# Attention scores computed with the keys as rows, exponentials read from PSUM without a shift, and a checked general path behind a branch

## The chip, the core and the metric

The kernel runs on one core of a Trainium2 chip. TensorE (PE) multiplies matrices and writes PSUM, VectorE (DVE) and ScalarE (ACT) work element by element, GpSimd (POOL) issues the gathers and scatters, SyncE (SP) and ACT issue the plain loads. The metric is the device time of one execution in microseconds (us), the median of several.

## The reference, cut to what matters

Attention over chunks of 32 queries feeds a mixture of experts in which each token goes to one expert. B, H, S, D are 4, 8, 768, 64; there are 8 memory keys per head, 8 experts, and F is 1024.

```python
for c in range(nc):                       # chunks of 32 queries
    l_start = max(0, c_start - 16); r_end = min(S, c_end + 8)
    k_full = concat([mem_k, k[:, :, l_start:r_end]]); v_full = ...   # same for v
    scores = (1 / sqrt(64)) * q_c @ k_full.T
    scores = scores - max(scores, axis=-1)
    a = exp(scores)
    a = a / (sum(a, axis=-1) + 1e-09)
    out[:, :, c_start:c_end] = a @ v_full
x = out in the form (B, S, 512)
logits = x @ w_gate                       # (B, S, 8)
local_gate = sigmoid(x @ w_local)         # below 0.5: take a fresh expert, else the one before
e = ...                                   # expert of the token, a scan along s
out[b, s] = softmax(logits)[e] * (relu(x @ w1[e]) @ w2[e])
```

## The kernel before, in words

Everything is fp32. There are two stages, one after the other, in `attention` and `experts`.

**Attention.** The 768 queries of a batch are cut into 8 blocks of 96 (three chunks each), 32 blocks in all. For a block, one band of 128 keys is used for every query: the 8 memory keys and 120 neighbours; a mask sets what a chunk may not see to -1e30. Loads come in units of half a batch (4 blocks): `load` fetches one `qt` of 768 KB, four bands of `kt` (240 KB each, the memory keys are copied in by POOL) and of `vt`, one unit ahead. For each block:

- `scores` (L151): 8 matmuls `s_ps` at L155, one per head, with the queries as the stationary operand (64 rows, 96 columns) and the keys streaming (128 columns). The heads lie in pairs on the two halves of the 128 rows. DVE scales and masks all of it from PSUM to `s_sb` (L159), takes the negated maximum `nmax` (L163), and ACT makes the exponentials head by head, 8 instructions of 96x128, with `nmax` as bias (L165).
- `values` (L168), for each half of the heads: PE transposes `s_sb` into `pt_ps` (L172, four transposes), ACT copies that to `pt` (L174), PE multiplies it with the values, which carry a column of ones, into `o_ps` (L178), and DVE adds 1e-9 to the sums, inverts them and scales (L180 to L182) into `x`.
- `logits` (L186): PE transposes `x` into `xt_ps` (L189), DVE copies it to `xt` (L191), PE multiplies it with the gate's weights into `l_ps` (L194), DVE copies that to `lt` (L195).

The scores of a block are asked for one block ahead, inside a unit. After each batch, `route` (L197) finds the expert of each token: DVE makes a code per token, PE turns the codes into a line (`c_ps`, L222, twice), DVE scans along the 768 tokens (`run` L226, `rank` L233, L237), PE turns the ranks back (`r_ps`, L240), and POOL scatters the rows of `x` to `x_dram` with 8 indirect DMAs, each of which waits for the one ahead of it (L263).

**Experts.** From the counts of tokens a plan of tiles of 128 tokens is made. Each tile gathers its rows (`xs`, L366), loads the two weights of its expert (`w_sb`, 2 MB each, four buffers ahead, L370 and L372), transposes (`g_ps`), multiplies (`h_ps` L391, `y_ps` L396) and scatters the result (`out_dram`, L399). 24 tiles always run; up to 7 more stand in nested branches on the number of tiles, which each engine reads into a register (L360). Here 27 run.

The order of the instructions on each engine is made by a scheduler when the program is built; each engine then works strictly through its own list. PSUM has 8 banks: `s_ps` holds two buffers of two, `pt_ps` two of one, `o_ps` one, and `xt_ps`, `l_ps`, `c_ps` and `r_ps` share one.

Of the kernel before, what the change touches and what calls it, by code (L numbers as in the profile page):

```python
# [15 lines left out]
P = 128  # L16
# [23 lines left out]
WBUF = 4  # L40


GATE = -1.5 * 2.0 ** -23
# [6 lines left out]
@with_exitstack  # L50
def kernel(
    ctx: ExitStack,
    tc: tile.TileContext,
    q: bass.AP,
    k: bass.AP,
    v: bass.AP,
    mem_k: bass.AP,
    mem_v: bass.AP,
    w_gate: bass.AP,
    w_local: bass.AP,  # L60
    w1: bass.AP,
    w2: bass.AP,
    out: bass.AP,
):
    nc = tc.nc
    keep = ctx.enter_context(tc.tile_pool(name="keep", bufs=1))
    dram = ctx.enter_context(tc.tile_pool(name="dram", bufs=1, space=bass.MemoryType.DRAM))
    x_dram = dram.tile([E * REGION, XW], I32, name="x_dram")

    ident = keep.tile([P, P], F32, name="ident")  # L70
    make_identity(nc, ident)
    count = keep.tile([E, 1], F32, name="count")

    attention(tc, q, k, v, mem_k, mem_v, w_gate, w_local, x_dram, ident, count)
    experts(tc, x_dram, out, ident, count, w1, w2)


@with_exitstack
def attention(ctx, tc, q, k, v, mem_k, mem_v, w_gate, w_local, x_dram, ident, count):

    nc = tc.nc
    once = ctx.enter_context(tc.tile_pool(name="once", bufs=1))
    ld = ctx.enter_context(tc.tile_pool(name="ld", bufs=2))
    sp = ctx.enter_context(tc.tile_pool(name="sp", bufs=2))
    xp = ctx.enter_context(tc.tile_pool(name="xp", bufs=2))
    sm = ctx.enter_context(tc.tile_pool(name="sm", bufs=3))
    sps = ctx.enter_context(tc.tile_pool(name="sps", bufs=2, space=PSUM))
    tps = ctx.enter_context(tc.tile_pool(name="tps", bufs=2, space=PSUM))
    ops = ctx.enter_context(tc.tile_pool(name="ops", bufs=1, space=PSUM))
    xps = ctx.enter_context(tc.tile_pool(name="xps", bufs=1, space=PSUM))  # L90

    memk = once.tile([P, B, HP, NMEM], F32, name="memk")
    nc.scalar.dma_start(memk, mem_k)

    def load(b, half):
        qt = ld.tile([P, HP, HQ], F32, name="qt")
        nc.sync.dma_start(qt, q[b, half])
        kt = ld.tile([P, HALF, HP, P], F32, name="kt")
        nc.gpsimd.tensor_copy(kt[:, :, :, 0:NMEM], memk[:, b:b + 1].to_broadcast([P, HALF, HP, NMEM]))
        vt = ld.tile([P, HALF, H * VW], F32, name="vt")  # L100
        for j in range(HALF):
            s0 = band_start(HALF * half + j)
            nc.sync.dma_start(kt[:, j, :, NMEM:P], k[b][:, :, s0:s0 + BAND])
            nc.scalar.dma_start(vt[0:NMEM, j], mem_v[b])
            nc.scalar.dma_start(vt[NMEM:P, j], v[b, s0:s0 + BAND])
        return qt, kt, vt

    units = [(b, half) for b in range(B) for half in range(2)]
    loaded = {units[0]: load(*units[0])}

# [3 lines left out]

    masks = {}
    for name, qb in (("first", 0), ("mid", 1), ("last", NQB - 1)):
        m = masks[name] = once.tile([QB, P], F32, name=f"mask_{name}")
        nc.vector.memset(m, MASKED)
        nc.vector.memset(m[:, 0:NMEM], 0.0)
        for g in range(QB // CHUNK):  # L120
            c0 = QB * qb + CHUNK * g
            lo = max(c0 - LEFT, 0) - band_start(qb) + NMEM
            hi = min(c0 + CHUNK + RIGHT, S) - band_start(qb) + NMEM
            nc.vector.memset(m[CHUNK * g:CHUNK * g + CHUNK, lo:hi], 0.0)

# [23 lines left out]

    def scores(qt, kt, half, j):  # L150
        s_ps = sps.tile([QB, 2, HP, P], F32, name="s_ps")  # L151
        for a in range(HP):
            for u in range(2):
                h = slice(DH * u, DH * u + DH)
                nc.tensor.matmul(s_ps[:, u, a], lhsT=qt[h, a, QB * j:QB * j + QB], rhs=kt[h, j, a],  # L155
                                 start=True, stop=True)
        s_sb = sp.tile([QB, H, P], F32, name="s_sb")
        m = mask_of(HALF * half + j)
        nc.vector.scalar_tensor_tensor(  # L159
            s_sb, s_ps.rearrange("p u a n -> p (u a) n"), SCALE,  # L160
            m.rearrange("p (o n) -> p o n", o=1).to_broadcast([QB, H, P]), ALU.mult, ALU.add)
        nmax = sm.tile([QB, H], F32, name="nmax")
        nc.vector.tensor_reduce(nmax, s_sb, axis=AX.X, op=ALU.max, negate=True)  # L163
        for i in range(H):
            nc.scalar.activation(s_sb[:, i], s_sb[:, i], ACT.Exp, bias=nmax[:, i:i + 1])  # L165
        return s_sb

    def values(s_sb, vt, j, x):  # L168
        for u in range(2):
            pt_ps = tps.tile([P, HP, QB], F32, name="pt_ps")  # L170
            for a in range(HP):
                nc.tensor.transpose(pt_ps[:, a], s_sb[:, HP * u + a], identity=ident[:QB, :QB])  # L172
            pt = sp.tile([P, HP, QB], F32, name="pt")
            nc.scalar.copy(pt, pt_ps)  # L174
            o_ps = ops.tile([QB, HP, VW], F32, name="o_ps")
            for a in range(HP):
                h = 2 * a + u
                nc.tensor.matmul(o_ps[:, a], lhsT=pt[:, a], rhs=vt[:, j, VW * h:VW * h + VW], start=True, stop=True)  # L178
            rinv = sm.tile([QB, HP, 1], F32, name="rinv")
# [6 lines left out]
    def logits(x, lt):  # L186
        xt_ps = xps.tile([P, DK, QB], F32, name="xt_ps", tag="xps")
        for kk in range(DK):
            nc.tensor.transpose(xt_ps[:, kk], x[:, P * kk:P * kk + P], identity=ident[:QB, :QB])  # L189
        xt = sp.tile([P, DK, QB], F32, name="xt")  # L190
        nc.vector.tensor_copy(xt, xt_ps)  # L191
        l_ps = xps.tile([QB, E + 1], F32, name="l_ps", tag="xps")
        for kk in range(DK):
            nc.tensor.matmul(l_ps, lhsT=xt[:, kk], rhs=wg[:, kk], start=(kk == 0), stop=(kk == DK - 1))  # L194
        nc.vector.tensor_copy(lt, l_ps)  # L195
# [70 lines left out]

    for n, (b, half) in enumerate(units):
        if n + 1 < len(units):
            loaded[units[n + 1]] = load(*units[n + 1])
        if half == 0:  # L270
            x = xp.tile([QB, NQB, XW], F32, name="x")
            lt = sm.tile([QB, NQB, E + 1], F32, name="lt")
        qt, kt, vt = loaded.pop((b, half))
        held = scores(qt, kt, half, 0)
        for j in range(HALF):
            ahead = scores(qt, kt, half, j + 1) if j + 1 < HALF else None
            values(held, vt, j, x[:, HALF * half + j])
            logits(x[:, HALF * half + j], lt[:, HALF * half + j])
            held = ahead
        if half == 1:  # L280
            route(b, x, lt)


# [167 lines left out]
```

## Time and profile before

| | us |
|---|---|
| median of 3 runs | 842.08 (836.47 to 842.37) |
| the profiled execution, its own time | 847.82 |
| its span, first to last instruction | 846.1 |
| PE busy | 706.1 |
| DVE busy | 205.1 |
| ACT busy | 160.4 |
| mean granted TensorE clock | 0.749 |

The span is cut into 40 slices of some 21 us on the page; a digit is the busy share of an engine in tenths. The attention takes about the first 17 of the slices. PE runs each fp32 matmul as two passes, so the 256 matmuls of `s_ps` are 512 in the profile, and a transpose as one. A group's line gives engine, operation, tile, shape and count, then busy time and the mean of one in ns, then the idle time ahead of it and what ended it. In the chain of waits each piece is what the end of the program hung on at that time.

### The profile page before, as it was taken

To read this page: it belongs to the slowest core of one execution; us is meant where nothing else is said; L and a number is where in the kernel's file an instruction comes from. 1 tells how busy PE (TensorE), PEld (TensorE's weight loads), DVE (VectorE), ACT (ScalarE), POOL (GpSimd) and SP (SyncE) were. 2 spreads that over 40 slices of the span, in tenths; PEclk is the share of its full clock that TensorE was granted. 3 is DMA by queue.
4 is the path that set the end of the run, shared out by engine and by line. 5 is a ranking of instruction groups with operands and counts; after the bars stand their busy time and mean duration, and the time that the engine had idled before them with its cause. 6 is when DMAs were issued, how large, how long until landed. Compare 5 with 4: busy or idle time off the path is not lost.

```text
span 846.1 us, 10132 instructions
## 1 busy us (share of the span) xinstructions
PE 706.1 (83%) x4064; PEld 556.5 (66%) x4064; DVE 205.1 (24%) x522; ACT 160.4 (19%) x406; POOL 87.8 (10%) x111
## 2 busy tenths in 40 slices
PE   3999898989898977301899999999999999997663
PEld 3788778878887777300686767777686777756551
DVE  3445464547454743600000000000000000000000
ACT  1524233322332341000011111111111111110000
POOL 1000002100200020022010101011010101000000
PEclk9555555555555555555799999999999999997887
DMA  9430405140601010027999988888888888850000
GB/s 249 108 108 28 131 4 170 41 135 10 173 29 51 10 58 10 0 60 293 428 425 423 376 313 323 314 301 326 328 319 321 325 318 300 309 202 23 26 25 3
DMA packets 38273, 156.41 MB, mean 185 GB/s; under 512 B 21261, under 2 KB 21389, under 8 KB 31312
## 3 DMA queue, kind: packets, MB, share of 16 engines
q1 hardware_dynamic: 25824, 127.41, 40.8%
q0 software_dynamic: 6368, 19.72, 6.5%
q10 hardware_dynamic: 6032, 8.61, 3.8%
q8 instruction: 34, 0.56, 0.3%
q14 instruction: 15, 0.12, 0.1%
HBM read 143.11 MB, written 13.39 MB: 185 GB/s over the span
## 4 chain that ended last, share of the span: by engine, by line
PE 61%; issue 13%; DMA 13%; DVE 8%; ACT 1%; POOL 1%; ACTq 0%; POOLq 0%; DVEq 0%
PE h_ps L391 16%; PE y_ps L396 15%; PE o_ps L178 9%; PE s_ps L155 7%; DMA out_dram<-y,to 5%; PE pt_ps L172 5%; PE l_ps L194 4%; DMA xs<-x_dram,rows 3%; PE xt_ps L189 3%; DMA x_dram<-x,row 3%; PE c_ps L222 1%; PE r_ps L240 1%; DVE s_sb L159 1%; DMA vt<-in_v_dram 1%; DVE x L182 1%
## 5 line engine op out<-in xcount | busy, mean ns | idle before, releaser
L391 PEld LDWEIGHTS h_ps<-xt,w_sb 128*128 128x128 f32 x1728 | 204.2, 198 | 15.6 <-DVE xt L380 8.2
L391 PE MATMUL h_ps<-xt,w_sb 128*128 128x128 f32 x1728 | 206.7, 282 | 5.8 <-DVE xt L380 5.0
L396 PE MATMUL y_ps<-w_sb,ht 128*128 128x512 f32 x432 | 189.9, 592 | 0.0
L396 PEld LDWEIGHTS y_ps<-w_sb,ht 128*128 128x128 f32 x432 | 80.0, 190 | 90.4 <-issue 90.4
L178 PE MATMUL o_ps<-vt,pt 128*96 128x65 f32 x512 | 95.1, 364 | 5.8 <-DVE x L182 4.4
L178 PEld LDWEIGHTS o_ps<-vt,pt 128*96 128x96 f32 x512 | 88.2, 277 | 13.9 <-issue 10.6
L382 DVE TENSOR_TENSOR to<-xs,past 128x1 int32<-128x1 f32 x27 | 4.3, 159 | 370.0 <-DMA out_dram<-y,to 224.8
L155 PE MATMUL s_ps<-kt,qt 64*96 64x128 f32 x512 | 78.0, 437 | 13.6 <-POOL place L309 8.0
L165 ACT ACTIVATE s_sb<-s_sb,nmax 96x128 f32<-96x128 f32 x256 | 80.5, 390 | 31.5 <-DVE nmax L163 31.5
L393 ACT ACTIVATE ht<-h_ps 128x512 f32<-128x512 f32 x54 | 32.2, 597 | 270.8 <-PE h_ps L391 270.8
L155 PEld LDWEIGHTS s_ps<-kt,qt 64*96 64x96 f32 x512 | 57.2, 267 | 24.6 <-issue 8.1
L378 PE MATMUL g_ps<-ident,xs 128*128 128x128 f32 x108 | 18.0, 313 | 64.6 <-DMA xs<-x_dram,rows 64.6
L172 PE MATMUL pt_ps<-ident,s_sb 96*128 96x96 f32 x256 | 60.6, 378 | 11.0 <-ACT pt L174 6.9
L399 POOL DMA_INDIRECT out_dram<-y,to x27 | 27.3, 1013 | 386.7 <-ACT y L398 352.7
L378 PEld LDWEIGHTS g_ps<-ident,xs 128*128 128x128 f32 x108 | 14.4, 161 | 73.5 <-issue 64.1
L174 ACT COPY pt<-pt_ps 128x384 f32<-128x384 f32 x64 | 30.5, 478 | 151.8 <-PE o_ps L178 112.3
L172 PEld LDWEIGHTS pt_ps<-ident,s_sb 96*128 96x128 f32 x256 | 44.7, 230 | 21.0 <-ACT pt L174 11.2
L263 POOL DMA_INDIRECT x_dram<-x,row x32 | 29.6, 925 | 247.3 <-DVE x L260 171.6
L398 ACT ACTIVATE y<-y_ps,xs 128x512 f32<-128x512 f32 x27 | 18.6, 688 | 170.9 <-PE y_ps L396 164.6
L194 PEld LDWEIGHTS l_ps<-wg,xt 128*96 128x96 f32 x256 | 44.8, 280 | 1.8 <-DVE xt L191 0.9
L194 PE MATMUL l_ps<-wg,xt 128*96 128x9 f32 x256 | 43.8, 301 | 0.7 <-DVE xt L191 0.7
L163 DVE TENSOR_REDUCE nmax<-s_sb 96x8 f32<-96x1024 f32 x32 | 38.3, 1198 | 0.1
(97 smaller groups left out, 303.0 us busy)
## 6 DMA issues: line engine op xcount, KB each, us to landing
w_sb<-in_w_dram SPq DMA_DIRECT2D x54, 2048.0 KB
vt<-in_v_dram ACTq DMA_DIRECT2D x32, 243.8 KB
kt<-in_k_dram SPq DMA_DIRECT2D x32, 240.0 KB
qt<-in_q_dram SPq DMA_DIRECT2D x8, 768.0 KB
vt<-in_mem_v_dram ACTq DMA_DIRECT2D x32, 16.2 KB
x_dram<-x,row POOLq DMA_INDIRECT x32, 3.2
xs<-x_dram,rows POOLq DMA_INDIRECT x27, 6.8
out_dram<-y,to POOLq DMA_INDIRECT x27, 7.5
```

Of the source, the lines that this page charges most:

```text
L155: nc.tensor.matmul(s_ps[:, u, a], lhsT=qt[h, a, QB * j:QB * j + QB], rhs=kt[h, j, a], start=True, stop=True)
L163: nc.vector.tensor_reduce(nmax, s_sb, axis=AX.X, op=ALU.max, negate=True)
L165: nc.scalar.activation(s_sb[:, i], s_sb[:, i], ACT.Exp, bias=nmax[:, i:i + 1])
L172: nc.tensor.transpose(pt_ps[:, a], s_sb[:, HP * u + a], identity=ident[:QB, :QB])
L174: nc.scalar.copy(pt, pt_ps)
L178: nc.tensor.matmul(o_ps[:, a], lhsT=pt[:, a], rhs=vt[:, j, VW * h:VW * h + VW], start=True, stop=True)
L194: nc.tensor.matmul(l_ps, lhsT=xt[:, kk], rhs=wg[:, kk], start=(kk == 0), stop=(kk == DK - 1))
L263: nc.gpsimd.indirect_dma_start(out=x_dram[:, :], out_offset=bass.IndirectOffsetOnAxis(ap=row[:, n:n + 1], axis=0), in_=x[:, n].bitcast(I32 ...
L378: nc.tensor.transpose(g_ps[:, kk], xs[:, P * kk:P * kk + P], identity=ident)
L391: nc.tensor.matmul(h_ps[:, m], lhsT=w1_sb[:, kk, P * (g + m):P * (g + m) + P], rhs=xt[:, kk], start=(kk == 0), stop=(kk == DK - 1))
L393: nc.scalar.activation(ht[:, g:g + 4], h_ps, ACT.Relu)
L396: nc.tensor.matmul(y_ps, lhsT=ht[:, m], rhs=w2_sb[:, m], start=(m == 0), stop=(m == FK - 1))
```

## The change

The host now lays out, for each of the 32 blocks, its queries, the band of 128 keys with the memory keys in it, and the values in the same way, so that a block is three plain loads (`qt` 196 KB, `kt` 262 KB, `vt` 266 KB), three blocks ahead, in four buffers. The scores of a block are made with the keys as the stationary operand, so that they come out with the keys as rows: the form that the value product needs. ACT reads them from PSUM and writes the exponentials to `pt`, three instructions of 128 rows by 256 elements (one for each chunk of 32 queries, over all heads), with the scale in the instruction and the mask as a bias per key; no maximum is taken off. The transposes `pt_ps`, their copies, the scaling and masking, the maximum and the addition of 1e-9 are gone. `o_ps` of all 8 heads stands in two banks and is inverted by one instruction and scaled by two. The copy of `xt_ps` goes from DVE to ACT. `s_ps` keeps two buffers of two banks, `o_ps` has two banks, `xt_ps` one of its own, and `l_ps`, `c_ps` and `r_ps` share one. All inverted sums are kept, counted at the end of the attention if they lie between 2^-40 and 2^40, and the count goes to a register of each engine after the experts. If it isn't 24576, the whole of attention and experts runs again in the form of before; that second program stands behind the branch.

```diff
     attention(tc, q, k, v, w_gate, w_local, x_dram, ident, count, kept_i)
     experts(tc, x_dram, out, ident, count, w1, w2)
+    kept = nc.values_load(kept_i, min_val=0, max_val=NT * H, skip_runtime_bounds_check_because="a count of sums")
+    with tc.If(kept < NT * H):
+        attention(tc, q, k, v, w_gate, w_local, x_dram, ident, count, None)
+        experts(tc, x_dram, out, ident, count, w1, w2)
...
-    ld = ctx.enter_context(tc.tile_pool(name="ld", bufs=2))
+    ld = ctx.enter_context(tc.tile_pool(name="ld", bufs=4))
...
+    def load(n):
+        qt = ld.tile([P, HP, QB], F32, name="qt")
+        nc.sync.dma_start(qt, q[n])
+        kt = ld.tile([P, HP, P], F32, name="kt")
+        nc.sync.dma_start(kt, k[n])
+        vt = ld.tile([P, H, VW], F32, name="vt")
+        nc.scalar.dma_start(vt, v[n])
         return qt, kt, vt
+    AHEAD = 3
+    loaded = {n: load(n) for n in range(AHEAD)}
...
+    def scores(qt, kt, qb):
+        s_ps = sps.tile([P, 2, 512], F32, name="s_ps")
+        st = s_ps[:, :, 0:HP * QB].rearrange("p u (a n) -> p u a n", a=HP)
         for a in range(HP):
             for u in range(2):
                 h = slice(DH * u, DH * u + DH)
-                nc.tensor.matmul(s_ps[:, u, a], lhsT=qt[h, a, QB * j:QB * j + QB], rhs=kt[h, j, a],
-                                 start=True, stop=True)
+                nc.tensor.matmul(st[:, u, a], lhsT=kt[h, a], rhs=qt[h, a], start=True, stop=True)
+        pt = sp.tile([P, 2, HP, QB], F32, name="pt")
+        m = mask_of(qb)
+        for g in range(NG):
+            c = slice(CHUNK * g, CHUNK * g + CHUNK)
+            nc.scalar.activation(pt[:, :, :, c], st[:, :, :, c], ACT.Exp, bias=m[:, g:g + 1], scale=SCALE)
+        return pt
+    def values(pt, vt, n, x):
+        o_ps = ops.tile([QB, 2, 512], F32, name="o_ps")
+        ot = o_ps[:, :, 0:HP * VW].rearrange("p u (a d) -> p u a d", a=HP)
+        for u in range(2):
+            for a in range(HP):
+                nc.tensor.matmul(ot[:, u, a], lhsT=pt[:, u, a], rhs=vt[:, 2 * a + u], start=True, stop=True)
+        rinv = rinvs[:, n]
+        nc.vector.reciprocal(rinv, ot[:, :, :, DH])
+        for u in range(2):
+            nc.vector.tensor_tensor(
+                x[:, 0:D].rearrange("p (a u d) -> p u a d", u=2, d=DH)[:, u], ot[:, u, :, 0:DH],
+                rinv[:, u].rearrange("p (a o) -> p a o", o=1).to_broadcast([QB, HP, DH]), op=ALU.mult)
...
     def logits(x, lt):
-        xt_ps = xps.tile([P, DK, QB], F32, name="xt_ps", tag="xps")
+        xt_ps = tps.tile([P, DK, QB], F32, name="xt_ps")
...
-        nc.vector.tensor_copy(xt, xt_ps)
+        nc.scalar.copy(xt, xt_ps)
...
+    begun = begin(0)
+    for n in range(NB):
...
+        ahead = begin(n + 1) if n + 1 < NB else None
+        make_values(*begun, n, x[:, j])
+        logits(x[:, j], lt[:, j])
+        begun = ahead
+        if j == NQB - 1:
             route(b, x, lt)
+    if not shifted:
+        flat = rinvs.rearrange("p n u a -> p (n u a)")
+        ok = once.tile([QB, NB * H], F32, name="ok")
+        nc.vector.tensor_scalar(ok, flat, 1.0 / SAFE, None, ALU.is_ge)
+        nc.vector.scalar_tensor_tensor(ok, flat, SAFE, ok, ALU.is_le, ALU.mult)
+        kept = once.tile([QB, 1], F32, name="kept")
+        nc.vector.tensor_reduce(kept, ok, axis=AX.X, op=ALU.add)
...
+        nc.tensor.matmul(k_ps, lhsT=kept, rhs=every, start=True, stop=True)
+        nc.vector.tensor_copy(kept_i, k_ps)
```

The form of before is kept as `shifted_scores` and `shifted_values` for the second program; the route and the experts are unchanged.

How this orders PE in the middle of a batch: the first list is of before, a stretch in the second half of the first batch; a row is one run of matmuls into a tile, with the count of matmuls in the program.

```order
L178 MATMUL o_ps<-vt,pt 96x65 x4
L155 MATMUL s_ps<-kt,qt 96x128 x3
L172 MATMUL pt_ps<-ident,s_sb 128x96 x4
L155 MATMUL s_ps<-kt,qt 96x128 x2
L189 MATMUL xt_ps<-ident,x 128x96 x4
L178 MATMUL o_ps<-vt,pt 96x65 x4
L155 MATMUL s_ps<-kt,qt 96x128 x4
L194 MATMUL l_ps<-wg,xt 96x9 x4
L172 MATMUL pt_ps<-ident,s_sb 128x96 x4
L155 MATMUL s_ps<-kt,qt 96x128 x5
```

The second is of the change, one block in the third batch, with the semaphores that each row waits for; every block there has this pattern.

```order
L183 MATMUL s_ps<-qt,kt 128x96 [waits DMAHW4_49,DMAHW3_49]
L183 MATMUL s_ps<-qt,kt 128x96 x7
L240 MATMUL xt_ps<-ident,x 128x96 [waits DVE_49,PE_49]
L240 MATMUL xt_ps<-ident,x 128x96 x3
L196 MATMUL o_ps<-vt,pt 96x65 [waits DMAHW5_49,PE_49]
L196 MATMUL o_ps<-vt,pt 96x65 x5
L245 MATMUL l_ps<-wg,xt 96x9 [waits Activation_49]
L245 MATMUL l_ps<-wg,xt 96x9 x3
L196 MATMUL o_ps<-vt,pt 96x65 x2
```

The scores in this piece are those of two blocks ahead, `o_ps` is of the next block, `xt_ps` and `l_ps` of the present one; the transposes of the exponentials, which stood at four places of a unit between them, are gone.

ACT in the same place, one block: three exponentials, the copy of `xt_ps`, and the issue of a later block's values, all in one queue.

```order
L188 ACTIVATE pt<-s_ps,mask_last 128x8x32 [waits Activation_49]
L188 ACTIVATE pt<-s_ps,mask_last 128x8x32 x2
L242 COPY xt<-xt_ps 128x384 [waits PE_49,Activation_49]
L109 DMA vt<-in_v_dram 128x520 [waits DMAHW6_49,DMAHW2_49,PE_49]
L188 ACTIVATE pt<-s_ps,mask_first 128x8x32 [waits Activation_49]
```

Before, this queue held 8 exponentials and two copies of `pt_ps` in their place.

PE at the route behind the second batch, in the change:

```order
L183 MATMUL s_ps<-qt,kt 128x96 x9
L273 MATMUL c_ps<-ident,code 8x96 x4
L183 MATMUL s_ps<-qt,kt 128x96 x5
L273 MATMUL c_ps<-ident,code 8x96 x4
L183 MATMUL s_ps<-qt,kt 128x96 x3
L291 MATMUL r_ps<-ones,rank 96x1 x8
L240 MATMUL xt_ps<-ident,x 128x96 x4
L196 MATMUL o_ps<-vt,pt 96x65 x3
L245 MATMUL l_ps<-wg,xt 96x9 x4
L196 MATMUL o_ps<-vt,pt 96x65 x5
L240 MATMUL xt_ps<-ident,x 128x96 x4
```

Three matmuls of the scores stand between the second `c_ps` and `r_ps`, and on DVE the scaling of the block's `x` stands behind the whole scan. At the routes of the first and the third batch, 17 to 22 matmuls of the scores, 10 to 16 of `o_ps` and one or two sets of `xt_ps` stand there.

122 lines of the change are left out of this document (65 added, 57 removed).

## The prediction

> **What bounds the kernel now.** I read first the granted clock in the slices of the page and then the table of stretches, whose bounds I took from the first value product, the last logits, the first scatter of the last batch and the first product of the experts. In a row of the table stand the stretch, its length, the busy time and count of PE, PE's weight loads, DVE, ACT and POOL, then the granted clock, the DMA share and GB/s.
>
> ```profile
> PEclk9555555555555555555799999999999999997887
> ...
> 25.03:339.79 314.76, 282.48 (x1678) 245.75 (x1676) 159.16 (x397) 102.28 (x305) 23.70 (x29) 0.50 0.24 68
> 339.79:358.27 18.48, 6.44 (x36) 5.33 (x36) 12.10 (x39) 0.26 (x1) 0.00 (x1) 0.50 0.00 0
> 358.27:405.80 47.53, 3.29 (x13) 2.18 (x13) 4.58 (x16) 0.00 (x0) 11.16 (x12) 0.50 0.51 192
> 405.80:846.10 440.30, 402.92 (x2256) 294.20 (x2256) 19.63 (x49) 50.81 (x81) 49.64 (x50) 0.96 0.71 271
> ```
>
> The reader is to see four stages. In the first PE is busy 282 of 315 us, at half clock, with DVE at half and ACT at a third of the time: PE sets it. The second is the last route, a chain through DVE. The third is the scatter of the last batch and the first gathers and weights. The fourth is the experts, PE again. The change touches the first stage and what lies ahead of it, adds a little to the second, and puts something behind the fourth. So the next view is the chain of waits over one unit of four blocks.
>
> ```profile
> by line: PE o_ps L178 29.0%; PE s_ps L155 26.4%; PE pt_ps L172 17.6%; PE l_ps L194 12.9%; PE xt_ps L189 8.6%; DVE x L182 2.1%; ACT pt L174 1.3%; issue 1.0%; DVE rinv L181 0.5%; DVE rinv L180 0.5%; DVE lt L195 0.4%; ACTq L174 0.0%
> ...
> 139.61 1.96 PE s_ps L155 x16
> ...
> 143.96 0.90 PE xt_ps L189 x4
> 144.86 1.23 PE o_ps L178 x8
> 146.09 1.20 PE l_ps L194 x8
> ...
> 177.05 1.96 PE s_ps L155 x16
> ```
>
> From 139.61 to 177.05 four blocks take 37.44 us, 9.36 each. 94.5% of it is PE, 17.6% (1.65 us a block) transposes `pt_ps`, and some 5% waits for DVE and ACT.
>
> **The first stage, block by block.** Taken away from PE: 8 transposes a block. Left: 16 passes of `s_ps`, 16 of `o_ps`, 4 of `xt_ps`, 8 of `l_ps`. By the rows above, where they run in one piece: `o_ps` 2 x 1.23 = 2.46, `xt_ps` behind scores 0.90, `l_ps` 1.20. The scores swap their operands. A pass now loads 128 columns instead of 96 and streams 96 instead of 128, which no row shows on 64 rows. Its bounds: if the stream decides, 1.96 x 96/128 = 1.47; if the load decides, 16 passes at the 0.15 us of the experts' first products (128 columns loaded, on 128 rows, at half clock; rows below), 2.4. I take 1.96, the row of the same tile with the same operands. Sum 6.52; the order lists a switch less often than before, and I add 0.1 for handovers: 6.6 a block. The upper bound keeps the whole fragmentation of before: 9.36 less the 17.6% and less the 5.8% of waits, 7.2.
>
> It holds only if nothing else takes longer than PE. ACT: three exponentials and a copy.
>
> ```profile
> 24.75 2.45 ACT L165 ACTIVATE s_sb<-s_sb,nmax 96x128 f32<-96x128 f32 x8
> ...
> L174 ACT COPY pt<-pt_ps 128x384 f32<-128x384 f32 x64 | 30.5, 478 | 151.8 <-PE o_ps L178 112.3 <-PE pt_ps L172 23.1 <-DMA vt<-in_v_dram 8.5
> ...
> L393 ACT ACTIVATE ht<-h_ps 128x512 f32<-128x512 f32 x54 | 32.2, 597 | 270.8 <-PE h_ps L391 270.8
> ...
> L182 DVE TENSOR_TENSOR x<-o_ps,rinv 96x256 f32<-96x256 f32 x64 | 26.6, 416 | 1.1
> ```
>
> Eight exponentials of 128 take 2.45, so 0.306 each; from 384 to 512 elements an ACT instruction grows by 119 ns, 0.93 an element, so 256 cost 0.306 + 0.119 = 0.43, three 1.28, with the copy 1.76 a block of 6.6. DVE has two of 0.42 and an inversion that I put at 0.2 (it is shorter than half of such a row): 1.0, and small copies. In the order of the change, 8 matmuls of scores (1.96) stand between the end of `o_ps` and its `xt_ps`, longer than DVE's 1.0 plus handovers; between `xt_ps` and `l_ps` stand 12 passes of `o_ps`, 1.85, while ACT needs what is left of its exponentials (1.28 less 0.90) and 0.48. So both are covered, ACT by about 1 us: if that cover goes, `l_ps` waits and the block ends at PE plus the lack. The removed work of DVE (scale, mask, maximum) and the second of ACT's copies ran beside PE; I count it only in the waits that go, 0.54 a block, already left out.
>
> Three routes lie inside this stage. Their `c_ps`, twice each, and `r_ps` stay on PE; the rows are those of the last.
>
> ```profile
> 343.52 1.46 PE c_ps L222 x8
> ...
> 352.34 2.68 PE r_ps L240 x16
> ```
>
> 2 x 1.46 + 2.68 = 5.6, three times 16.8. Between the end of the second `c_ps` (344.98) and `r_ps` lie 7.36 us of DVE. At the routes of the first and third batch the order puts 17 to 22 matmuls of scores and 10 or more of `o_ps` there, 6 us and more; I count 1.5 each for what DVE delivers late. At the second only 3 matmuls, 0.8 us, so 6.5 are idle; and since the scaling of that block's `x` is queued on DVE behind the scan, `xt_ps` starts 0.6 late and the next one, with no scores ahead of it, 1.2: 8.3. At the first blocks, before the order is in step, 1.5; at the last three, where no scores are left to cover DVE, 4.2. Waits together 17. The stage: 32 x 6.6, less 3.9 for two scores done ahead of it, plus 16.8 and 17: 241 instead of 315.
>
> **The start.** Loads of half a batch give way to loads of a block.
>
> ```profile
> 0.00:12.00 12.00, 3.35 (x28) 3.03 (x30) 4.21 (x19) 0.00 (x0) 2.97 (x19) 1.00 0.86 235
> ...
> 17.92 1.28 ACT L165 ACT_TABLE_LOAD   x1 [17.92 <-DMA vt<-in_v_dram]
> ...
> 25.03 1.54 PE L178 MATMUL o_ps<-vt,pt 128*96 128x65 f32 x8
> ```
>
> ACT's queue was held by the issue of values until 17.92. Three blocks are now 2.2 MB, 9.3 us at the 235 GB/s of the first stretch, and the issue of the fourth values, which waits for one of the first loads, stands ahead of the table load: I put that at 8, plus 1.28 and the exponentials 1.28, first value product at 11, between 9 and 15, instead of 25.
>
> **The second and third stages.** The check adds three DVE instructions, which run while the last `xt_ps` and `l_ps` do, and in the last route one matmul and one copy: 0.5, so 19. The last eight scatters, the gathers, the weights and the experts keep their order and their waits: nothing. First scatter at 11 + 241 + 19 = 271 instead of 358, 87 less.
>
> **The end.** Each engine reads the count and branches.
>
> ```profile
> L360 POOLq TENSOR_LOAD <-total_i x1: 513/513/513, 760.9 to 760.9; - x1
> ...
> _compat.py:109 PEldq COMPARE_BRANCH  x5: 65/92/3321, 754.6 to 832.7; - x5
> _compat.py:109 POOLq COMPARE_BRANCH  x5: 34/40/50, 761.5 to 838.0; - x5
> ```
>
> POOL is the last to be free there. A read of 0.51 and a branch of 0.04 are the lower bound, 0.55; the 3.32 of PE's longest branch, the one that leaves the last tile, with the read the upper, 3.8. I take 2. The Trainium skill, "Runtime: NRT & Kernel Launch", section "Instruction fetch mechanics", says that a taken branch to a target outside the window already fetched must wait for a fetch; by it the jump over the second program would sit at the upper bound, and the sum would be 2 us more. PE's 3.32 agrees; POOL's 0.05 doesn't show it.
>
> **The sum.** 87 - 2 = 85. The profiled execution's span goes from 846.1 to 761, its time from 847.8 to 763. The median of the runs shown, 842.08, lies 5.7 below that execution, so I forecast 757.
>
> **Rivals.**
>
> *The clock rises in the attention* (8%).
>
> ```profile
> 24.00:36.00 12.00, 12.00 (x79) 10.12 (x76) 7.29 (x13) 6.59 (x21) 0.00 (x0) 0.50 0.45 121
> ...
> 409.00:410.00 1.00, 1.00 (x7) 0.50 1.04 442
> ...
> 412.00:413.00 1.00, 1.00 (x11) 1.00 1.08 459
> ```
>
> The experts' first passes ran at 0.50, about 0.15 us each, and 4 us of them brought the clock to 1.00 and 0.09 to 0.11 a pass. In the attention 12 us of busy PE did not. If a mix without `pt_ps` did, a block would cost about 0.72 x 6.6 = 4.8, with 1.8 x 32 = 58 less: 700. Against it: the stream's share of a pass hardly grows. The Trainium skill, "TensorE: Matmul & The Clock Gate", Part 1, has the clock go to full after about 3.4 us of sustained work, and Part 4 says that transposes don't count as such work in the same way; by these the change, which takes away two thirds of the transposes, could be enough. The row from 24 to 36, with most of its time in other matmuls, speaks against it.
>
> *PE waits for DVE and ACT in each block* (6%). If exponentials from PSUM by strides of 32 cost what the row of a 512-wide one does, 0.6 each, and DVE's handovers take 1 us more, `l_ps` and `xt_ps` come late by 1 to 1.5 a block: 32 to 48 us, 790 to 805.
>
> *Loads take over* (2%), the case that ends slower. ACT's next exponentials are queued behind the issue of a block's values, which waits for loads of some three blocks back. A block is 0.725 MB.
>
> ```profile
> 17.00:18.00 1.00, 0.00 (x0) 1.00 1.07 224
> ```
>
> At the 224 GB/s of a stretch in which the DMA engines were full, that is 3.2 us, under half a block. It would decide from 6.6 us (110 GB/s), and the kernel would be slower than before by 1% from 9.5 us a block, below 77 GB/s, at 855 or more. Larger pieces than before speak against it.
>
> *The change doesn't do what it says* (2%). If the count falls short, the second program runs as well: 757 and about 840, near 1600. The inputs are a tenth of a unit normal, so scores are near 0 and a sum is that of 48 to 64 terms near 1; nothing comes near 2^40. If the swapped scores cost more than the transposes saved, the result is within 1% (2%).
>
> **How the numbers follow.** The forecast has 80%; its own range: low, with the scores at 1.47 (16 less) and the start at 9, 739; high, with 7.2 a block (19 more), the start at 15 and the branch at 3.8, 782. For 8 in 10 I widen the low side for half of a risen clock: 730 to 785. Faster by over 1% (about what a measurement of this kernel can tell from no change) is 0.95: the forecast, the clock and the waits; within 1% 0.02; slower 0.03, the loads and a second program.
>
> **What would show it.** Right: no `pt_ps`; first `o_ps` near 11; a block near 6.6 us in the chain with PE over 95% of it; a clock of 0.50; an idle PE of 6 to 8 us before `r_ps` only at the second route; first scatter of the last batch near 271; 490 us from there to the end. Wrong: `s_ps` passes of 0.15 us or more, `l_ps` idle behind ACT's copy, or an end that stretches by more than 4 us.

## The result, and the profile after

| | before | changed |
|---|---|---|
| median, us | 839.49 (836.47 to 842.37, 4 runs) | 767.77 (766.81 to 768.29, 4 runs) |
| ratio, 95% interval | | 0.9145 (0.9101 to 0.9189) |
| profiled execution, own time and span | 847.82, 846.1 | 768.29, 766.6 |

The changed kernel is faster by 8.6%. The forecast of 757 was 11 us too low; 768 lies inside the range of 730 to 785.

First the same table of stretches as before, now of the changed kernel, with the bounds at the same events: first value product, last logits, first scatter of the last batch, first product of the experts; then the stretch from the issue of the last `out_dram` to the end.

```profile
10.25:254.76 244.51, 231.66 (x1474) 216.05 (x1472) 65.53 (x214) 52.86 (x128) 22.18 (x24) 1.00 0.35 104
254.76:273.19 18.43, 6.56 (x38) 5.42 (x38) 12.09 (x40) 0.26 (x1) 0.00 (x0) 1.00 0.00 0
273.19:321.00 47.81, 4.23 (x17) 3.12 (x18) 4.59 (x16) 0.00 (x0) 11.17 (x12) 1.00 0.53 201
321.00:766.60 445.60, 401.23 (x2253) 292.52 (x2252) 19.64 (x49) 50.80 (x81) 49.34 (x50) 0.96 0.70 267
747.10:766.60 19.50, 0.00 (x0) 0.00 (x0) 0.00 (x0) 0.00 (x0) 0.99 (x1) 0.59 0.02 5
```

The same last stretch of the kernel before:

```profile
833.54:846.10 12.56, 0.00 (x0) 0.00 (x0) 0.00 (x0) 0.00 (x0) 1.00 (x1) 0.65 0.01 2
```

Stage by stage, the span changes by: start 10.25 - 25.03 = -14.8; attention 244.5 - 314.8 = -70.3; last route 0.0; first scatter of the last batch to the last `out_dram` 473.9 - 475.3 = -1.4; end 19.5 - 12.6 = +6.9. Together -79.5, from 846.1 to 766.6.

The chain of waits of the changed kernel behind the second route: start, length, what.

```profile
136.29 1.39 PE c_ps L273 x8
...
138.29 1.76 DVE run L277
...
141.87 1.81 DVE rank L284
...
145.04 2.70 PE r_ps L291 x16
...
158.84 1.96 PE s_ps L183 x16
160.79 0.83 PE xt_ps L240 x4
161.63 1.87 PE o_ps L196 x12
163.50 1.19 PE l_ps L245 x8
164.68 0.73 PE o_ps L196 x4
165.42 1.96 PE s_ps L183 x16
```

A block is now 165.42 - 158.84 = 6.58 us, all of it PE: five runs of passes follow one another without a gap. The 7.36 us of DVE between the end of `c_ps` (137.68) and `r_ps` are there as well; PE works on six passes of the scores at their beginning and is idle for 6.27 of them.

One row of the page looks as if the clock had risen: the attention stood at 5 before, and stands at 9 now.

```profile
PEclk9999999999999999999999999999999999988985
```

But the passes have the same length as before: 1.96 for sixteen of `s_ps`, 1.19 for eight of `l_ps` (1.20 before). Either these passes don't feel the clock, or the row is wrong. The runs below decide that.

### The profile page after: what moved, and what is told of

The parts are those of the page before. It is cut to its first block, busy times and chain, and to the rows that moved or that the text cites. A ratio compares the mean times of both kernels' runs of the same rounds, so it can differ in the third digit from the quotient of the medians.

```text
span 766.6 us, 9247 instructions
## 1 busy us (share of the span) xinstructions
PE 647.7 (84%) x3810; PEld 520.7 (68%) x3810; DVE 103.6 (14%) x332; ACT 106.4 (14%) x214; POOL 85.3 (11%) x106
## 4 chain that ended last, share of the span: by engine, by line
issue 32%; PE 31%; DMA 31%; DVE 3%; POOL 0%; POOLq 0%; ACT 0%; SPq 0%; ACTq 0%; DVEq 0%
DMA out_dram<-y,to 24%; PE o_ps L196 11%; PE s_ps L183 8%; PE l_ps L245 5%; PE xt_ps L240 4%; DMA x_dram<-x,row 3%; DMA xs<-x_dram,rows 3%; PE c_ps L273 1%; PE r_ps L291 1%; DMA kt<-in_k_dram 1%; DVE x L200 1%; DVE rank L284 0%; DVE run L277 0%; POOL out_dram L468 0%; DVE rank L288 0%
## 5 line engine op out<-in xcount | busy, mean ns | idle before, releaser
L183 PE MATMUL s_ps<-qt,kt 64*128 64x96 f32 x512 | 72.1, 435 | 6.8 <-DMA kt<-in_k_dram 6.3
L183 PEld LDWEIGHTS s_ps<-qt,kt 64*128 64x128 f32 x512 | 61.8, 323 | 12.4 <-issue 8.5
L188 ACT ACTIVATE pt<-s_ps,mask_mid 128x256 f32<-128x256 f32 x72 | 29.4, 471 | 68.5 <-PE s_ps L183 35.8
L240 PE MATMUL xt_ps<-ident,x 96*128 96x96 f32 x128 | 29.4, 380 | 5.4 <-DVE x L200 5.3
L242 ACT COPY xt<-xt_ps 128x384 f32<-128x384 f32 x32 | 15.3, 478 | 92.0 <-PE xt_ps L240 88.2
L435 POOL DMA_INDIRECT xs<-x_dram,rows x27 | 26.1, 967 | 11.1 <-issue 8.0
L240 PEld LDWEIGHTS xt_ps<-ident,x 96*128 96x128 f32 x128 | 19.9, 219 | 10.9 <-issue 10.2
```

The costliest lines, as they stand in the source:

```text
L183: nc.tensor.matmul(st[:, u, a], lhsT=kt[h, a], rhs=qt[h, a], start=True, stop=True)
L188: nc.scalar.activation(pt[:, :, :, c], st[:, :, :, c], ACT.Exp, bias=m[:, g:g + 1], scale=SCALE)
L435: nc.gpsimd.indirect_dma_start(out=xs.bitcast(I32), out_offset=None, in_=x_dram[:, :], in_offset=bass.IndirectOffsetOnAxis(ap=rows[:, i:i ...
```

## The experiments

### The end: is the longer end the branch?

The theory was that most of the 6.9 us are steps which POOL takes one after the other at the branch, whose body is skipped. These are the sequencers' rows of line 81 of the changed kernel, the branch: shortest, median and longest in ns, then the first and last start in us.

```profile
L81 POOLq EVENT_SEMAPHORE  x6: 17/30/43, 756.2 to 756.6; - x6
...
L81 PEldq COMPARE_BRANCH  x1: 3820/3820/3820, 746.9 to 746.9; - x1
...
L81 POOLq COMPARE_BRANCH  x1: 55/55/55, 753.4 to 753.4; - x1
L81 POOLq INC_SWDGE_SEM  x1: 1881/1881/1881, 756.7 to 756.7; - x1
```

POOL compares at 753.4, is seen next at 756.2, and is done at 758.6, 8.0 us ahead of the end. Before, POOL's last step of that kind ended at 838.0, 8.1 ahead of the end. The branch's own length on POOL is 0.055 us; the 2.8 us show only as a gap behind it, ahead of its first semaphore step.

The changed kernel was run again beside its variants.

> The changed kernel unaltered, run beside its variants. Both theories: 767 to 768.5 us, a granted clock of 1.00 through the attention, and 19 to 20 us from the issue of the last out_dram (L468) to the end of the span.

Measured 769.69 us (766.47 to 770.74), a little above what was expected; its end took 19.2 us.

**Without the branch.**

```diff
-    kept = nc.values_load(kept_i, min_val=0, max_val=NT * H, ...)
-    with tc.If(kept < NT * H):
-        attention(tc, q, k, v, w_gate, w_local, x_dram, ident, count, None)
-        experts(tc, x_dram, out, ident, count, w1, w2)
```

> The changed kernel without L80 to L83: the count of kept sums is still made and never read, and the general program behind it is left out (the data here don't need it). Theory: the end grew by 6.9 us (19.5 us from the last out_dram to the end of the span, 12.6 before), and 5.8 us of it are POOL's own steps at the untaken branch, one after the other: the read and compare (752.8 to 753.4), the jump (753.4 to 756.2) and the semaphore step with its INC_SWDGE_SEM of 1.88 us (756.2 to 758.6). Without them the end is 12.5 to 14 us and the time 768 - 5.8 = 762. Rival: the longer end isn't the branch's but the last scatter's landing or the code's size elsewhere; then the end stays at 19 and the time at 767 to 768.

Measured 761.02 us (759.99 to 763.13), 8.7 below the run beside it. The last stretch of this kernel, from its last `out_dram`:

```profile
746.55:759.10 12.55, 0.00 (x0) 0.00 (x0) 0.00 (x0) 0.00 (x0) 0.99 (x1) 0.64 0.01 4
```

12.55 against 12.56 before: the whole of the longer end is the branch with what stands behind it. Some 3 us of the difference between the two profiled spans lie elsewhere (the last `out_dram` was issued at 746.55 here, at 749.81 in the run beside it and at 747.10 in the first profile of the changed kernel); that is the spread from one execution to the next.

**A small body behind the branch.**

```diff
     with tc.If(kept < NT * H):
-        attention(tc, q, k, v, w_gate, w_local, x_dram, ident, count, None)
-        experts(tc, x_dram, out, ident, count, w1, w2)
+        nc.vector.memset(count, 0.0)
```

> The same read and the same branch, with one vector memset behind it in place of the general program (which is left out). If the distance of the jump is what costs, POOL's 2.8 us and PE's branch of 3.82 us shrink to under 0.3 us each, the end is 16.5 to 17 us and the time 765. If any branch costs it, nothing changes: 19.5 and 768. If the step with INC_SWDGE_SEM is there only because the body holds DMAs of POOL, it goes as well: 14 us and 762.5.

Measured 762.94 us (761.79 to 764.97). This run doesn't tell the two theories apart: the body writes only `count`, which the experts' plan has read by 271, and the scheduler put the branch ahead of the experts' tiles. Its rows show a branch over a short body, at 271.5 instead of the end.

```profile
L81 POOLq COMPARE_BRANCH  x1: 50/50/50, 271.5 to 271.5; - x1
L81 PEldq COMPARE_BRANCH  x1: 239/239/239, 271.5 to 271.5; - x1
```

In the next two runs the body writes `out`, and the branch stayed at the end.

**One DMA behind the branch, from SP.**

```diff
     with tc.If(kept < NT * H):
-        attention(tc, q, k, v, w_gate, w_local, x_dram, ident, count, None)
-        experts(tc, x_dram, out, ident, count, w1, w2)
+        nc.sync.dma_start(out[0:1, 0:1], ident[0:1, 0:1])
```

> The same read and branch at the end, with one 4-byte DMA of SP to out behind it in place of the general program (which is left out, and so is its need here), so that the branch stays where it was and the jump over its body is short. Theory (the distance costs on PE and POOL): PE's branch 3.82 -> 0.2 to 0.3 us, POOL's step from branch to semaphore 2.8 -> under 0.3 us, and, as POOL issues no DMA in the body, no INC_SWDGE_SEM: the end is 12.6 + 0.6 to 1 for the read = 13.2 to 13.7 us, the time 762 to 763. Rival (any branch at the end costs its 5.8 us): end 18 to 19.5 us, 768.

Measured 761.9 us (761.21 to 763.87). PE's branch and the end in this run:

```profile
L81 PEldq COMPARE_BRANCH  x1: 252/252/252, 748.9 to 748.9; - x1
```

```profile
749.08:762.10 13.02, 0.00 (x0) 0.00 (x0) 0.00 (x0) 0.00 (x0) 0.99 (x1) 0.64 0.01 4
```

A read and a branch over a short body cost 13.02 - 12.55 = 0.5 us.

**The same DMA from POOL.**

```diff
-        nc.sync.dma_start(out[0:1, 0:1], ident[0:1, 0:1])
+        nc.gpsimd.dma_start(out[0:1, 0:1], ident[0:1, 0:1])
```

> As the run with SP's DMA behind the branch, but the DMA is issued by POOL. Theory: a short jump here too, and the INC_SWDGE_SEM of 1.9 us comes back with a body that holds a DMA of POOL: end 15.5 to 16.5 us, the time 764.5 to 765.5, 2 to 3 us above the run with SP's DMA. Rival: the two are the same, and the INC_SWDGE_SEM belongs to the branch or to nothing that this tells.

Measured 764.42 us (763.68 to 765.01), with an end of 15.0 us and this row:

```profile
L81 POOLq INC_SWDGE_SEM  x1: 1861/1861/1861, 753.4 to 753.4; - x1
```

A body that holds a DMA of POOL costs 15.0 - 13.0 = 2.0 us when it is skipped. What is left, 19.2 to 19.5 less 15.0, 4.2 to 4.5 us, goes with the body of a whole second program. The rows of the changed kernel's trace divide it into three. First, 1.2 us lie ahead of the branch: POOL's semaphore steps behind the last `out_dram` run from 747.1 to 750.8, where the kernel before took from 833.5 to 836.0 (the row's line, in a helper, is that of the branches on the number of tiles).

```profile
_compat.py:109 POOLq EVENT_SEMAPHORE  x4: 17/42/43, 747.1 to 750.8; - x4
```

Why POOL waits longer there isn't shown; the traces of all kernels with the whole program behind a branch at the end have it, and no other. Second, 2.6 us are the gap between POOL's compare and its next step, 2.8 us here and under 0.2 in the run with POOL's DMA. The other engines have such a gap too, ACT from 747.7 to 750.8.

```profile
L81 ACTq EVENT_SEMAPHORE  x2: 17/17/17, 750.8 to 750.9; - x2
...
L81 ACTq COMPARE_BRANCH  x1: 55/55/55, 747.7 to 747.7; - x1
```

Third, the six semaphore steps take from 756.2 to 756.7, 0.5 us. So the number of semaphores is the small part and the gap behind the jump the large one; that the gap grows with the distance of the jump is argued from these bodies, not tested by several distances.

**The branch ahead of the experts.** The general path is then the shifted attention alone, and the experts stand once behind both.

```diff
     attention(tc, q, k, v, w_gate, w_local, x_dram, ident, count, kept_i)
-    experts(tc, x_dram, out, ident, count, w1, w2)
...
     with tc.If(kept < NT * H):
         attention(tc, q, k, v, w_gate, w_local, x_dram, ident, count, None)
-        experts(tc, x_dram, out, ident, count, w1, w2)
+    experts(tc, x_dram, out, ident, count, w1, w2)
```

> The branch moved ahead of the experts: behind it only the shifted attention, and the experts once, after it, for both cases. The end then has no L81 step: 12.5 to 14 us. Theory: the branch's steps on POOL are a chain wherever they stand, so the first gather xs of the experts, which POOL issues 4.0 us after the last scatter (296.81 to 300.84), comes 4 to 6 us later, and the time is 766 to 768.5. Rival: they hide under the landing of the scatters, the gather stays where it is and the time is 762.

Measured 762.62 us (761.62 to 764.33), 7.1 below the changed kernel beside it; ratio to before 0.9073 (0.9004 to 0.9143). The rival was nearly right: the end is 12.8 us, and the first gather comes at 301.68 (300.84 in the changed kernel), so most of the branch hides under the landing of the last scatter. Not all of it: from the last scatter to the first gather it is 5.9 us here (295.76 to 301.68) and 4.0 in the changed kernel (296.81 to 300.84). This version does everything that the changed kernel does.

**The plan's tables in memory of their own**, to win back what is left of that:

```diff
+    once = ctx.enter_context(tc.tile_pool(name="eonce", bufs=1))
+    pl = ctx.enter_context(tc.tile_pool(name="plan", bufs=1))
     attention(tc, q, k, v, w_gate, w_local, x_dram, ident, count, kept_i)
...
-    experts(tc, x_dram, out, ident, count, w1, w2)
+    experts(tc, x_dram, out, ident, count, w1, w2, once, pl)
```

> The version with the branch ahead of the experts, and the experts' plan and its tables in memory of their own, claimed ahead of the attention. Theory: in that version the plan's copy to total_i waited 16.7 us, until POOL's last scatter, for memory that the attention had held, and so the first gather came at 301.7 us instead of 300.8; with memory of its own the plan is made under the scatters as in the changed kernel, the gather comes 3.5 to 4.3 us after the last scatter, and the time is 760.5 to 761.5. Rival: the plan waits for the branch on POOL whatever memory it has (no row shows a DVE step of the plan before 296), and the time stays at 762.6.

Measured 762.85 us (761.13 to 763.82): no gain. The plan's wait of 16.7 us is gone, as the theory said, but POOL's steps at the branch were right behind it: its compare at 295.7, its last semaphore at 298.7 with an INC_SWDGE_SEM of 0.8, and the gather at 300.43, 5.1 after the last scatter. That is 0.8 us less than with the shared memory and 1.1 more than in the changed kernel; a step of 0.8 is below what these medians can tell. Two waits had ended at nearly the same time, and removing one left the other.

### The attention: loads, transposes, cover

**The old arithmetic with the new loads.** The general path alone:

```diff
-    attention(tc, q, k, v, w_gate, w_local, x_dram, ident, count, kept_i)
+    attention(tc, q, k, v, w_gate, w_local, x_dram, ident, count, None)
     experts(tc, x_dram, out, ident, count, w1, w2)
-    kept = nc.values_load(kept_i, min_val=0, max_val=NT * H, ...)
-    with tc.If(kept < NT * H):
...
-    sps = ctx.enter_context(tc.tile_pool(name="sps", bufs=1 if shifted else 2, space=PSUM))
+    sps = ctx.enter_context(tc.tile_pool(name="sps", bufs=2, space=PSUM))
```

> The general path alone, with two buffers for its scores: the arithmetic of before (shift, transposes, two o_ps), with the new loads (one block each, four buffers, three ahead), the look ahead across units and no branch at the end. Theory: the loads are worth only the earlier start, the first value product at 14 to 17 us instead of 25, blocks stay at 9.3 to 9.8 us, clock 0.50: 828 to 834 us. Rival: the loads and the look ahead took the waits out of the blocks, and 8.3 us of PE work are left in each: 795 us or less.

Measured 824.4 us (821.77 and 827.03; before, beside it, 844.73; ratio 0.9768, 0.9637 to 0.9899). That is far from the rival's 795, and the loads are worth mainly the earlier start, as the theory had it, but its numbers missed: the time lies below 828, and the first value product comes at 17.73, later than 14 to 17 and 7.3 us earlier than before. The stage behind it takes nearly as long.

```profile
17.73:320.00 302.27, 274.38 (x1693) 233.08 (x1692) 145.28 (x367) 116.55 (x338) 22.18 (x24) 0.57 0.27 79
```

Its attention was 12.5 us shorter than 314.8. The granted clock here has a mean of 0.57, spells at 1.00 among 0.50, and those may be all of the 12.5; that stays open. So of the span's 79.5 us, 20.9 go to loads, order and such spells, and 65.5 to the arithmetic, less the 6.9 of the branch.

**Eight more transposes a block**, the number that the change removed, of `x` and read by nobody:

```diff
-        xt_ps = tps.tile([P, DK, QB], F32, name="xt_ps")
+        x_full = tps.tile([P, 512], F32, name="xt_ps")
+        xt_ps = x_full[:, 0:DK * QB].rearrange("p (k n) -> p k n", k=DK)
...
+        for kk in range(8):
+            nc.tensor.transpose(x_full[:, DK * QB:DK * QB + QB], x[:, P * (kk % DK):P * (kk % DK) + P],
+                                identity=ident[:QB, :QB])
```

> The changed kernel with eight more 96 x 128 transposes in each block (of the block's x, into the unused columns of xt_ps's bank, read by nobody), the number and shape that the change took out. Theory: the gain is PE's own work and the waits around it, so putting back the work alone gives back 8 x 0.21 us = 1.66 us a block (xt_ps: 0.83 us for 4), 53 us in all: 821 us, with blocks of 8.2 to 8.3 us; what is then still missing to 840 is the wait that went with pt_ps. And the transposes are what held the clock at 0.50: it falls from 1.00 to 0.50 in the attention, and s_ps x16 still takes 1.96 us. Rival 1: the clock stays at 1.00, so that it is not the transposes that set it. Rival 2: a lower clock does lengthen the passes (s_ps x16 beyond 2.2 us), so that part of the gain was clock; then the time is over 830.

Measured 796.08 us. In its chain a block runs from 108.25 to 116.11:

```profile
108.25 1.96 PE s_ps L183 x16
110.21 0.84 PE xt_ps L241 x4
111.04 1.28 PE xt_ps L243 x8
112.32 1.55 PE o_ps L196 x10
113.87 1.19 PE l_ps L248 x8
115.06 1.05 PE o_ps L196 x6
116.11 1.96 PE s_ps L183 x16
```

7.86 us instead of 6.58: eight transposes are 1.28, not 1.66. I had taken 0.21 from a run of four, which carries the start of a run on another tile; in a longer run one costs 0.16. The kernel grew by 28 us, not by 32 x 1.28 = 41. In part that is because the added work fills idle time of PE (`r_ps` of the second route no longer waits): the stage has 5.3 us of it here and 12.9 in the changed kernel.

```profile
10.35:283.00 272.65, 267.34 (x1728) 253.01 (x1728) 65.17 (x214) 53.11 (x128) 22.18 (x24) 1.00 0.32 93
```

So putting the transposes' PE time back returns 28 of 65 us of the arithmetic. Some 37 are left between this run and the old arithmetic with the new loads, and the two rows of the stage say where: 7.4 ahead of the first value product (17.73 less 10.35), 22.6 in PE's idle time (302.27 less 274.38 is 27.9; here 5.3), 7.0 in PE's busy time. Before the change PE waited in this stage for DVE's `x` (12.3 us), DVE's codes and lines (7.5), ACT's copies `pt` (8.3) and DVE's `s_sb` (3.5). Which of the removed steps is worth how much of the 22.6 was not tested one by one.

**The same with plain products** (`nc.tensor.matmul` in place of `nc.tensor.transpose`, same operands):

> As the run with eight more transposes a block, but as plain products of the same x with the same identity (two passes each of the size of those of s_ps, 0.122 us a pass). Block 6.6 + 8 x 0.245 = 8.5 us, 768 + 63 = 831 us. If it is the transposes as such that hold the clock low, the clock stays at 1.00 here; if it is the amount of work on PE, it falls here as there.

Measured 865.19 us: slower than before by 2.5% (ratio 1.0251, 1.0136 to 1.0366). The sixteen passes cost 3.41 us a block:

```profile
155.08 3.42 PE xt_ps L243 x16
```

That is 0.213 a pass, not the 0.122 that I had taken from `s_ps`. `s_ps` works on 64 of the 128 rows, two heads on the two halves in turn; these products use 96 rows as one. A price of a pass can't be carried from one form to another. A transpose of the same operands, 0.16, is a single pass.

**Exponentials twice.**

```diff
             nc.scalar.activation(pt[:, :, :, c], st[:, :, :, c], ACT.Exp, bias=m[:, g:g + 1], scale=SCALE)
+            nc.scalar.activation(pt[:, :, :, c], st[:, :, :, c], ACT.Exp, bias=m[:, g:g + 1], scale=SCALE)
```

> The changed kernel with each exponential computed twice (the same values written again): 1.41 us more of ACT's work in each block, 3.3 instead of 1.9 of 6.6 us. Theory (exponentials and the copy of x lie under PE's work, and the copy stands in ACT's queue behind no more than four of them, with 0.8 us to spare): 768 to 772 us, no idle PE before l_ps. Rival: the copy comes later by more than it has, l_ps waits 0.6 us in each block: 787 us or more.

Measured 766.62 us, no slower than the changed kernel. `l_ps` in this run:

```profile
L246 PE MATMUL l_ps<-wg,xt 128*96 128x9 f32 x256 | 44.6, 304 | 0.6 <-ACT xt L243 0.6
```

0.6 us of waiting for the copy in the whole program: the exponentials and the copy lie under PE with room for 1.4 us more a block.

### The clock: a gauge in the attention

```diff
+        if n in (12, 20, 28):
+            for kk in range(32):
+                nc.tensor.matmul(x_full[:, DK * QB:512], lhsT=ident, rhs=ident, start=True, stop=True)
```

(`x_full` as in the run with eight transposes; `logits` is given the block's number `n`.)

> The changed kernel with a gauge for the clock at three places of the attention (blocks 12, 20 and 28): 32 products of the shape of the experts' h_ps (128 x 128 by 128 x 128, 64 passes, of the identity with itself) into the unused columns of xt_ps's bank, read by nobody. In the experts such a group of 64 takes 7.31 us where the profile's clock row and its records say 1.00, and 8.83 to 9.17 us as the first group, which began ahead of the trace's first record of the clock in the changed kernel, and at 0.50 in the kernel before. Theory: the 1.00 of the page through the changed attention is only the absence of a record, the clock there is that of before; each group takes 8.8 to 9.2 us and the run 768 + 27 = 795 us. Rival: the clock is 1.00 there, and the attention's passes don't feel it; each group takes 7.2 to 7.4 us.

Measured 752.01 us in a single execution, with work added that PE spent 26 us on: *faster* than the changed kernel by 16 us (before, beside it: 838.6 to 847.9). Neither theory had that. In order of time, PE's groups of this run around the first gauge:

```profile
97.38 1.39 PE L249 MATMUL l_ps<-wg,xt 128*96 128x9 f32 x8
...
107.22 8.47 PE L244 MATMUL xt_ps<-ident 128*128 128x128 f32 x64
...
117.65 1.14 PE L183 MATMUL s_ps<-qt,kt 64*128 64x96 f32 x16
118.89 0.53 PE L241 MATMUL xt_ps<-ident,x 96*128 96x96 f32 x4
119.26 1.16 PE L196 MATMUL o_ps<-vt,pt 128*96 128x65 f32 x12
120.25 0.80 PE L249 MATMUL l_ps<-wg,xt 128*96 128x9 f32 x8
120.90 0.53 PE L196 MATMUL o_ps<-vt,pt 128*96 128x65 f32 x4
121.36 1.14 PE L183 MATMUL s_ps<-qt,kt 64*128 64x96 f32 x16
```

Ahead of the gauge eight passes of `l_ps` take 1.39 us, behind it 0.80; sixteen of `s_ps` 1.14, where the changed kernel's trace has 2.03 in this view. A block takes 121.36 - 117.65 = 3.71 us instead of 6.58. So these passes do feel the clock, and the table of stretches says 1.00 on both sides of the gauge:

```profile
100.00:107.20 7.20, 7.20 (x45) 6.71 (x45) 1.28 (x5) 1.68 (x4) 1.60 (x2) 1.00 0.51 156
...
115.50:120.05 4.55, 4.44 (x56) 4.24 (x56) 1.12 (x4) 2.16 (x5) 1.21 (x2) 1.00 0.42 111
120.05:145.00 24.95, 21.85 (x245) 20.01 (x243) 14.47 (x45) 8.17 (x21) 1.83 (x2) 0.97 0.70 206
145.00:154.18 9.18, 9.18 (x61) 8.89 (x60) 1.58 (x7) 2.04 (x5) 1.84 (x2) 0.50 0.38 96
```

The first 1.00 is wrong; the passes there have the length of the row with 0.50. The lengths change while the first gauge runs, the trace's records of the clock begin only there, and ahead of the first record the page fills in full speed. The changed kernel shows the same by itself, in its experts: its first record of the clock lies at 324.1, and the first tile's products, begun ahead of it at a 1.00 that is filled in, take 8.83 us, the second tile's 7.31.

```profile
320.94 8.83 PE L460 MATMUL h_ps<-xt,w_sb 128*128 128x128 f32 x64
...
336.48 7.31 PE L460 MATMUL h_ps<-xt,w_sb 128*128 128x128 f32 x64
```

The other two gauges (8.19 and 9.27 us in this view, so also begun at the low clock) did the same. The chain shows how long their passes are ahead of the rise:

```profile
211.57 3.47 PE xt_ps L244 x16
```

That is 0.217 us a pass, against 7.31 / 64 = 0.114 at full clock. A group that stays at the low clock would take 64 x 0.217 = 13.9 us (an estimate), not the 8.8 to 9.2 that the theory counted with: the groups that it took them from had the rise of the clock inside them, and so has each gauge. By the trace's records the high clock lasted until 143.7, 194.9 and 225.6, each time within some 15 us of PE's first waits of about 1 us for DVE or ACT. The changed kernel thus ran its attention at the clock of before.

## Why the prediction was right, and where it was off

- **A block of 6.6.** Measured 6.58. The scores with swapped operands were taken at 1.96, between 1.47 and 2.4, and took 1.96. The row of the old form was taken without a reason why neither the shorter stream nor the longer load should count, and no run shows one; that it fitted to the digit is luck. The bound of 2.4 was too low, as its 0.15 us a pass was (see the clock, below; at 0.217 it would have been 3.5). `o_ps` was 2.60 (2.46 forecast), `xt_ps` 0.83 (0.90), `l_ps` 1.19 (1.20).
- **ACT and DVE covered.** An exponential of 256 took 0.47 (0.43 forecast). Doubling them cost nothing, so the cover is at least the 1 us that was claimed.
- **The stage of 241.** Measured 244.5. The idle time before `r_ps` at the second route was 6.27, forecast 6.5. Part of the 3.5 lies in the first batch, whose blocks took 7.0 instead of 6.6.
- **The start at 11 and the tail of 19.** Measured 10.25 and 18.43. First scatter of the last batch forecast at 271, measured 273.19. The start came out near 11 by another path: ACT's table load began at 6.29, not at 8, and the exponentials were done at 9.0; then the value product still stood behind the second block's scores, which PE did from 8.30 to 10.32 when their keys had landed.
- **Nothing for scatters, gathers and experts.** Measured 1.4 us less. That step held.
- **The end, +2.** This is the term that was mis-sized: measured +6.9, outside the bounds of 0.55 to 3.8. The bounds counted a read and one branch on POOL, or PE's longest branch. The runs show in place of them 0.5 for a read and a short branch, 2.0 because the skipped body holds DMAs of POOL, and some 4.3 that come with a whole program as the body: a gap of 2.6 behind POOL's compare, 0.5 of semaphore steps, and 1.2 that POOL waits longer ahead of the branch. The rule of the Trainium skill, "Runtime: NRT & Kernel Launch", section "Instruction fetch mechanics", that a taken branch out of the fetched window waits for a fetch, was closer than my choice: PE's branch of 3.82 over the whole program and 0.25 over one DMA agree with it. I had set it aside because POOL's row said 0.05; on POOL the time stands behind the row, as a gap of 2.8. That the gap is a fetch no run shows.
- **5.7 off for the median.** Wrong in size too: the changed kernel's profiled execution lies 0.5 above its median. Before's executions run from 835.8 to 847.9 us, with the mean clock falling from 0.768 to 0.747 along the way (in all but one of 17, whose 847.33 us stand beside a mean of 0.894); the profiled one was at the long end. The spread went with the clock, and need not carry over to another kernel. Together with the end and the stage this makes the 11 us.
- **The clock.** The rival of a risen clock did not come, though the page looks as if it had, and the argument against it, that busy PE alone had not raised the clock from 24 to 36, held. Its price was far too small: the kernel would have been near 700 by 4.8 us a block; at full clock a block is 3.71, 0.56 of 6.58 and not 0.72. The 0.72 rests on counting 7 passes of `h_ps` in 1 us of the low clock, 0.15 each. That view counts every pass that reaches into the window, and passes overlap; they follow one another at 0.21 us at the low clock and 0.11 at the high one. The 9.17 us of that group of 64, and the 8.83 after the change, are a mixture of both.
- **Loads, waits per block, the general path.** None of these rivals came. By the list of rivals the chances add up to 0.94 for faster and 0.04 for slower, not 0.95 and 0.03.

## What to carry to other kernels

Price a step by the pass lengths of the same form, and read a clock from pass lengths too: the clock row means nothing ahead of the trace's first record. A skipped body costs by what it holds, and more when it is a whole program, so put a rare path where its exit lies beside another wait; here that was worth 7 us. Where PE sets the time of a stage with small products, measure once with a dense group in it whether the stage runs at the low clock at all.

## What the runs showed of the hardware

- PE without a gap is not enough for the full clock: the changed kernel's stretch from 160 to 205 us has PE busy for 45.00 of 45.00 us, at blocks of 6.58. The Trainium skill, "TensorE: Matmul & The Clock Gate", Part 1, has the low clock as the default, which agrees, and the full one after about 3.4 us of sustained work, which that stretch doesn't show; with 128 x 128 products it came 1.8 to 4.0 us after a group's first pass (by the clock records of the gauges and of the experts before and after).

```profile
160.00:205.00 45.00, 45.00 (x300) 42.22 (x299) 8.46 (x37) 11.15 (x28) 4.58 (x5) 1.00 0.48 136
```

- In that single execution the gauges' 26 us of products for nobody saved 42 us of other work (768 + 26 - 752). If all 32 blocks ran at 3.71, that would be 32 x 2.87 = 92 us less (an estimate, with the routes unchanged). A kernel with such a group near the start and one behind each route, and the branch ahead of the experts, wasn't tried; what exactly raises and lowers the clock stays open, as does whether the removed transposes have any part in it, since the run with more of them had only the filled-in 1.00 and the low clock's pass lengths.
